# Gated mix of one decode step of cached attention and a feed-forward layer: from the tile framework to planned semaphores, with one TensorE loop over items, two key buffers and one value buffer

## The chip, the cores and the metric

The kernel runs on one core of a Trainium2 chip. The metric is the device time of one execution in microseconds (us). A core has five engines with instruction streams of their own: TensorE (PE in the profile; PEld are its weight loads), VectorE (DVE), ScalarE (ACT), GpSimd (POOL) and SyncE (SP). SP issues nearly all loads here, on one queue, which 16 DMA engines serve. An engine waits for another, or for a load, by a semaphore.

## The reference

All data is float32. B = 2 rows of x, D = 640, H = 32 heads of 128, 4096 cached positions, F = 1728.

```python
def _A_ref(x, k_cache, v_cache, wq, wo):            # x (2,1,640), caches (2,32,4096,128)
    q = (x @ wq).reshape(B, Sq, H, Dh)              # wq (640, 4096)
    scores = einsum("bhqd,bhkd->bhqk", q, k_cache) * Dh ** -0.5
    p = softmax(scores)
    o = einsum("bhqk,bhkd->bhqd", p, v_cache)
    return o.reshape(B, Sq, H * Dh) @ wo            # wo (4096, 640)

def _B_ref(x, w1, w2):                              # w1 (640, 1728), w2 (1728, 640)
    return silu(x @ w1) @ w2

g = sigmoid((x * gate_w).sum(-1))
out = g * _A_ref(...) + (1 - g) * _B_ref(...)
```

The caches are 268 MB of the 298 MB that are read.

## The kernel before

An *item* is four heads of one row of x: 16 items, `items[i] = (hq, b)`, with hq from 0 to 7 and b 0 or 1. For each item a key slab and a value slab of 128 partitions x 16384 floats (8.39 MB) are read. Everything large goes through three buffers of that size that rotate (`slabs`, SLOTS = 3): two loads with the query weights and w1, then keys and values, one load "mid" with w2 and the first two of eight groups of output weights, and at the very end "end" with the other six groups. The list `stream` sets the order, and all of them are issued on SP (`load` at L100, `load_wo` at L91). A load of the stream is issued once the one three places earlier has been used up (`spend`, `pump`): the framework makes it wait for the last reader of that buffer.

For an item, `products` multiplies the key slab by the query in place: VectorE the first 68 of 128 columns of 128 (L323), GpSimd the others (L320). `scores` sums them on VectorE (L331), `peak` finds each row's maximum (L336 to L340), and `weights` takes exponentials on ScalarE (L346) into `pz`, of which there are two. `total` and `values` run on TensorE: the sum of the exponentials (L357) and 32 products of 32 columns with the value slab (L372). `combine` scales the result on VectorE (L384) and picks each head's own part in one product (L394); `turn` adds and transposes once per pair of items (L405, L406). `project` multiplies by the output weights (L213): the groups up to the sixth into `early`, two strips of output partitions of 320 columns, and the last two into `acc`, four strips of 160; `merge` adds the first to the second. In program order an iteration holds item i's products and item i-1's values. The last value slab comes in two halves. At the end VectorE copies `acc` (L455), and SP and ACT store one row each (L457).

The queries of an item pair are spread over the partitions just before they are needed (`query`, L308), `ffn_in` and `query_rows` run at the start (L244, L291), and `ffn_out` after item 5 (`middle`).

Of the kernel before, what the change touches and what calls it, by code (L numbers as in the profile page):

```python
# [1 line left out]

# [12 lines left out]
@with_exitstack  # L15
def tile_gated_decode(
    ctx: ExitStack,
    tc: tile.TileContext,
    x: bass.AP,
    kc: bass.AP,  # L20
    vc: bass.AP,
    wq: bass.AP,
    wo: bass.AP,
    w1: bass.AP,
    w2: bass.AP,
    gate: bass.AP,
    out: bass.AP,
):
    nc = tc.nc
# [5 lines left out]
    Q = 4  # L35
# [5 lines left out]
    FR = F // P  # L41
    FM = FR * P
    FT = F - FM
    QF = FM // Q
    SLOTS = 3
    SLAB = C * DH
    QD = Q * DH

    const = ctx.enter_context(tc.tile_pool(name="const", bufs=1))
    slabs = ctx.enter_context(tc.tile_pool(name="slabs", bufs=SLOTS))  # L50
    work = ctx.enter_context(tc.tile_pool(name="work", bufs=2))
    ps_q = ctx.enter_context(tc.tile_pool(name="ps_q", bufs=1, space=bass.MemoryType.PSUM))
    ps_r = ctx.enter_context(tc.tile_pool(name="ps_r", bufs=1, space=bass.MemoryType.PSUM))
    ps_pv = ctx.enter_context(tc.tile_pool(name="ps_pv", bufs=2, space=bass.MemoryType.PSUM))
    ps_o = ctx.enter_context(tc.tile_pool(name="ps_o", bufs=1, space=bass.MemoryType.PSUM))
    ps_s = ctx.enter_context(tc.tile_pool(name="ps_s", bufs=3, space=bass.MemoryType.PSUM))
    order = ctx.enter_context(tc.manual_schedule())
# [4 lines left out]
    N = len(items)  # L62
    MID = 5
    J0 = SLAB // (H * DH)
    W1_AT = (J - J0) * H * DH
    XG_AT = W1_AT + J * F
    W2T_AT = FR * D
    WO_MID = 2
    WO_AT = {}
    for grp in range(HQ):  # L70
        WO_AT[grp] = ("mid", W2T_AT + D + grp * Q * D) if grp < WO_MID else ("end", (grp - WO_MID) * Q * D)
# [10 lines left out]
    T = {}  # L82
    spent = set()
    nxt = [0]

    def load_wo(grp, t):
        at = WO_AT[grp][1]
        src = wo[grp * QD : (grp + 1) * QD, :].rearrange("(p n) d -> p (n d)", n=Q)
        cuts = (0, Q * D - D, Q * D) if grp == HQ - 1 else (0, Q * D)
        for c0, c1 in zip(cuts, cuts[1:]):  # L90
            nc.sync.dma_start(t[:, at + c0 : at + c1], src[:, c0:c1])  # L91

    def load(what, n, t):
        if what in ("k", "v"):
            hq, b = items[n]
            src = (kc if what == "k" else vc)[b, Q * hq : Q * hq + Q]
            src = src.rearrange("h s d -> (h s d)").rearrange("(p c) -> p c", p=P)
            step = SLAB // 2 if (what, n) == ("v", N - 1) else SLAB
            for c in range(0, SLAB, step):
                nc.sync.dma_start(t[:, c : c + step], src[:, c : c + step])  # L100
        elif what == "wq":
            src = wq.rearrange("(p j) n -> p (j n)", j=J)
            if n == 0:
                nc.sync.dma_start(t, src[:, :SLAB])
            else:
                nc.sync.dma_start(t[:, :W1_AT], src[:, SLAB:])
                nc.sync.dma_start(t[:, W1_AT : W1_AT + J * F], w1.rearrange("(p j) f -> p (j f)", j=J))
        elif what == "mid":
            for grp in range(WO_MID):
                load_wo(grp, t)  # L110
            nc.sync.dma_start(t[:, : FR * D], w2[:FM, :].rearrange("(p n) d -> p (n d)", n=FR))
            nc.sync.dma_start(t[:FT, W2T_AT : W2T_AT + D], w2[FM:, :])
        else:
            for grp in range(WO_MID, HQ):
                load_wo(grp, t)

    def pump():
        while nxt[0] < len(stream):
            m = nxt[0]
            if m >= SLOTS and stream[m - SLOTS] not in spent:  # L120
                return
            t = slabs.tile([P, SLAB], F32, tag="slab", name=stream[m][0])
            load(*stream[m], t)
            T[stream[m]] = t
            nxt[0] += 1

    def spend(what, n):
        spent.add((what, n))
        pump()

    pump()
    xg = T["wq", 1][: B + 1, XG_AT : XG_AT + D]
    nc.scalar.dma_start(xg[:B], x.rearrange("b s d -> (b s) d"))
    nc.scalar.dma_start(xg[B : B + 1], gate[None, :])

    ident = const.tile([P, P], F32, name="ident")
    make_identity(nc, ident)
    ones = const.tile([P, P], F32, name="ones")  # L140
    nc.vector.memset(ones, 1.0)
    fold = const.tile([P, 2 * Q, Q, 4], F32, name="fold")
    nc.vector.memset(fold, 0.0)
    for q in range(Q):
        nc.vector.memset(fold[q * QP : (q + 1) * QP, :, q, :], 1.0)
    sel = const.tile([P, 4 * Q], F32, name="sel")
    nc.vector.reduce_sum(sel, ident.rearrange("p (a b) -> p b a", b=32)[:, : 4 * Q, :], axis=AX.X)
    pick = const.tile([P, P + 1], F32, name="pick")
    nc.vector.memset(pick, 0.0)
    nc.vector.reduce_sum(pick[:, 1 : P + 1 : 32], sel.rearrange("p (q c) -> p q c", c=4), axis=AX.X)  # L150
    own = const.tile([P, 4], F32, name="own")
    nc.vector.reduce_sum(own, sel.rearrange("p (q c) -> p c q", c=4), axis=AX.X)
    spread = const.tile([P, B, P], F32, name="spread")
    for b in range(B):
        for q in range(Q):
            nc.vector.tensor_copy(
                spread[:, b, q * QP : (q + 1) * QP],
                ident[:, 32 * q + b : 32 * q + b + 1].to_broadcast([P, QP]),
            )
    xz = const.tile([P, J, 32], F32, name="xz")  # L160
    nc.gpsimd.memset(xz, 0.0)
    pz = []
    for i in range(2):
        t = const.tile([P, NG, 32], F32, name=f"pz{i}")
        nc.gpsimd.memset(t, 0.0)
        pz.append(t)

    g = const.tile([P, B], F32, name="g")
    gc = const.tile([P, B], F32, name="gc")
    hT = const.tile([P, FR, B], F32, name="hT")  # L170
    hTt = const.tile([FT, 1, B], F32, name="hTt")

    def gates():
        xT = ps_s.tile([P, 512], F32, tag="sm", name="xT")
        for j in range(J):
            nc.tensor.matmul(  # L176
                xT[:, j * (B + 1) : (j + 1) * (B + 1)],
                xg[:, j:D:J],
                ident[: B + 1, : B + 1],
                start=True,  # L180
                stop=True,
            )
        xT = xT[:, : J * (B + 1)].rearrange("p (j r) -> p j r", j=J)
        nc.vector.tensor_copy(xz[:, :, :B], xT[:, :, :B])  # L184
        gx = const.tile([P, B, J], F32, name="gx")
        for b in range(B):
            nc.vector.tensor_mul(gx[:, b, :], xT[:, :, B], xz[:, :, b])
        gp = const.tile([P, B], F32, name="gp")
        nc.vector.reduce_sum(gp, gx, axis=AX.X)
        gl = ps_s.tile([P, 512], F32, tag="sm", name="gl")  # L190
        nc.tensor.matmul(gl[:, :B], ones, gp, start=True, stop=True)
        ge = const.tile([P, B], F32, name="ge")
        nc.scalar.activation(ge, gl[:, :B], AF.Exp, scale=-1.0)
        nc.vector.tensor_scalar_add(ge, ge, 1.0)
        nc.vector.reciprocal(g, ge)
        nc.vector.tensor_scalar(gc, g, -1.0, 1.0, op0=ALU.mult, op1=ALU.add)

    G = 4  # L200
    W = D // G
    W2 = D // 2
    LAST = HQ - 2
    both = ps_o.tile([P, W2 + W], F32, name="acc")
    early, acc = both[:, :W2], both[:, W2:]
    count = {"early": 0, "late": 0}
    total_of = {"early": Q * LAST + FR + 1, "late": Q * (HQ - LAST) + 1}

    def accumulate(lhsT, w, to="early"):
        m = lhsT.shape[1]  # L210
        dst, width = (early, W2) if to == "early" else (acc, W)
        for n in range(D // width):
            nc.tensor.matmul(  # L213
                dst[32 * n : 32 * n + m, :],
                lhsT,
                w[:, n * width : (n + 1) * width],
# [5 lines left out]
    def merge():  # L222
        part = const.tile([64, W2], F32, name="part")
        nc.scalar.copy(part, early[:64, :])
        for n in range(G):
# [6 lines left out]
                stop=False,  # L232
            )
        count["late"] += 1

    def ffn_in():
# [242 lines left out]
```

## Time and profile before

| | |
|---|---|
| three runs | 701.09, 701.51, 707.64 us (median 701.51) |
| span of the profiled execution | 700.5 us |
| its own time beside the span | not given apart; the runs' median lies 1.0 us above the span |
| read from memory | 298.26 MB |
| busy | DMA queue of SP 98.7%; DVE 67%, POOL 38%, PE 32%, ACT 5% |

The span runs from the first to the last instruction. In the timeline a row has the start, the length, the engine, the line, the operation, output and inputs, and in brackets the idle time before it with what ended it. In the chain of work that ended last a row has start, length and what. In the list of waits stand the waiter, what it waited for, the total, the number and the longest. "SPq" is SP issuing a load, "to landing" the time from issue until the data is there.

### The profile page before, as it was taken

How to read it: one execution, taken by the hardware profiler on the slowest of the kernel's cores; microseconds unless marked ns; L12 is line 12 of the kernel's file. 1: busy time of each engine (PE TensorE's matmuls, PEld its weight loads, DVE VectorE, ACT ScalarE, POOL GpSimd, SP SyncE). 2: the span in 40 equal slices, each digit the busy share in tenths (PEclk: the TensorE clock that was granted, in tenths of full speed). 3: DMA queues.
4: the chain of work that ended last, by engine and by line, in shares of the span. 5: the costliest groups of instructions: out<-in, count | busy, mean ns of one | idle time of the engine just before them, and what ended most of it. 6: DMA issues, size and time to landing. Idle time of an engine off the chain costs nothing.

```text
span 700.5 us, 3603 instructions
## 1 busy us (share of the span) xinstructions
PE 224.3 (32%) x1496; PEld 71.7 (10%) x1496; DVE 468.6 (67%) x212; ACT 37.8 (5%) x143; POOL 265.8 (38%) x25
## 2 busy tenths in 40 slices
PE   1630060506041240852240506050321406060467
PEld 1110010101010010210010102010100102010112
DVE  2016949494958869495949597795949495786901
ACT  0000000101010100101010101010010101010010
POOL 1006244270908163453618090724426080715300
PEclk9975565756657575877575757566565757566689
DMA  9999999999999999999999999999999999999995
GB/s 416 401 451 419 427 465 423 423 427 457 427 427 434 449 424 430 417 421 438 430 439 434 434 427 443 438 427 427 446 434 427 423 453 431 427 427 449 411 422 222
DMA packets 6742, 298.50 MB, mean 426 GB/s; under 512 B 763, under 2 KB 771, under 8 KB 1094
## 3 DMA queue, kind: packets, MB, share of 16 engines
q1 hardware_dynamic: 6712, 298.26, 98.7%
q8 instruction: 12, 0.20, 0.1%
q14 instruction: 4, 0.03, 0.0%
q10 hardware_dynamic: 14, 0.01, 0.0%
HBM read 298.26 MB, written 0.01 MB: 426 GB/s over the span
## 4 chain that ended last, share of the span: by engine, by line
DMA 59%; DVE 24%; PE 14%; another core or an unknown queue 1%; ACT 0%; issue 0%; SPq 0%; DVEq 0%; ACTq 0%
DMA k<-in_A_k_cache_dram 34%; DMA v<-in_A_v_cache_dram 20%; DVE s L331 15%; PE pv L372 10%; DVE k L323 8%; DMA wq<-in_B_w_dram 5%; PE acc L213 2%; PE orow L394 1%; PE hr L244 1%; DVE osb L384 0%; ACT pz L346 0%; PE tot L357 0%; DVE rg L365 0%; DVE m L336 0%
## 5 line engine op out<-in xcount | busy, mean ns | idle before, releaser
L320 POOL TENSOR_TENSOR k<-k,qsb 128x7680 f32<-128x7680 f32 x16 | 263.1, 16447 | 387.7 <-DMA k<-in_A_k_cache_dram 387.7
L331 DVE TENSOR_REDUCE s<-k 128x68 f32<-128x8704 f32 (+1 forms) x32 | 276.3, 8676 | 0.0
L323 DVE TENSOR_TENSOR k<-k,q 128x8704 f32<-128x8704 f32 x16 | 147.5, 9221 | 136.3 <-DMA k<-in_A_k_cache_dram 126.1
L372 PE MATMUL pv<-v,pz 128*32 128x512 f32 x1024 | 145.4, 731 | 248.1 <-DMA v<-in_A_v_cache_dram 248.1
L372 PEld LDWEIGHTS pv<-v,pz 128*32 128x32 f32 x1024 | 36.8, 131 | 342.8 <-issue 227.2
L394 PE MATMUL orow<-osb,pick 128*128 128x512 f32 x32 | 22.8, 800 | 118.2 <-DVE osb L384 118.2
L346 ACT ACTIVATE pz<-s,nb 32x128 f32<-32x128 f32 x64 | 25.5, 398 | 585.7 <-DVE nb L340 585.1
L384 DVE SCALAR_TENSOR_TENSOR osb<-pv,rg,own 128x512 f32<-128x512 f32 x16 | 12.0, 747 | 22.6 <-PE pv L372 22.6
L263 DVE STREAM_TRANSPOSE turned<-hr 128x416 f32<-128x416 f32 (+1 forms) x2 | 0.8, 408 | 30.6 <-PE hr L252 30.6
L357 PE MATMUL tot<-rs,fold 128*128 128x1 f32 x32 | 5.8, 250 | 43.2 <-ACT pz L346 43.2
L394 PEld LDWEIGHTS orow<-osb,pick 128*128 128x128 f32 x32 | 5.8, 226 | 127.9 <-DVE osb L384 127.9
L308 PE MATMUL q<-qrow,spread 128*128 128x128 f32 x32 | 7.2, 359 | 25.7 <-DVE tot L362 18.0
L291 PE MATMUL qr<-wq,xz 128*32 128x512 f32 x80 | 10.5, 683 | 9.2 <-DMA wq<-in_A_wq_dram 9.2
L405 DVE TENSOR_REDUCE row<-orow 128x128 f32<-128x512 f32 x8 | 5.5, 691 | 11.6 <-PE orow L394 11.6
L213 PE MATMUL acc<-mid,hT 128*2 128x320 f32 x52 | 10.1, 563 | 8.6 <-DMA mid<-in_B_w_dram 8.6
L357 PEld LDWEIGHTS tot<-rs,fold 128*128 128x128 f32 x32 | 7.2, 235 | 54.3 <-ACT pz L346 51.2
L346 ACT ACTIVATION_READ_ACCUMULATOR pz<-s,nb 32x1 f32 x64 | 11.8, 184 | 0.0
L213 PE MATMUL acc<-end,oP 128*2 128x320 f32 (+2 forms) x128 | 11.1, 366 | 0.0
L308 PEld LDWEIGHTS q<-qrow,spread 128*128 128x128 f32 x32 | 5.4, 239 | 32.6 <-issue 23.1
L244 PE MATMUL hr<-wq,xz 128*32 128x416 f32 x40 | 6.1, 744 | 5.0 <-DMA wq<-in_B_w_dram 5.0
L455 DVE COPY ot<-acc 128x160 f32<-128x160 f32 x1 | 0.3, 323 | 11.0 <-PE acc L213 11.0
L184 DVE COPY xz<-xT 128x10 f32<-128x10 f32 x1 | 0.2, 169 | 9.1 <-PE xT L176 9.1
(55 smaller groups left out, 65.8 us busy)
## 6 DMA issues: line engine op xcount, KB each, us to landing
v<-in_A_v_cache_dram SPq DMA_DIRECT2D x2, 4096.0 KB, 38.3
end<-in_A_wo_dram SPq DMA_DIRECT2D x5, 1280.0 KB, 21.0
wq<-in_B_w_dram SPq DMA_DIRECT2D x1, 4320.0 KB, 37.6
mid<-in_B_w_dram SPq DMA_DIRECT2D x1, 4160.0 KB, 27.9
mid<-in_A_wo_dram SPq DMA_DIRECT2D x2, 1280.0 KB, 17.5
wq<-in_A_wq_dram SPq DMA_DIRECT2D x1, 2048.0 KB, 26.7
end<-in_A_wo_dram SPq DMA_DIRECT2D x1, 960.0 KB, 26.8
end<-in_A_wo_dram SPq DMA_DIRECT2D x1, 320.0 KB, 27.1
```

What stands on the lines that cost most here:

```text
L213: nc.tensor.matmul(dst[32 * n : 32 * n + m, :], lhsT, w[:, n * width : (n + 1) * width], start=(count[to] == 0), stop=(count[to] == total_ ...
L244: nc.tensor.matmul(rows[32 * c : 32 * c + 32, :QF], xz[:, j, :], w[:, j, c * QF : (c + 1) * QF], start=(j == 0), stop=(j == J - 1),)
L291: nc.tensor.matmul(ps[u][32 * q : 32 * q + 32, :], xz[:, j, :], w[:, u * half : (u + 1) * half, q, :], start=(j == 0), stop=(j == J - 1),)
L308: nc.tensor.matmul(qps[hq][:, b, :], spread[:, b, :], qrow[:, hq, :], start=True, stop=True)
L320: nc.gpsimd.tensor_mul(k[:, CV:, :], k[:, CV:, :], qsb[hq][:, b, None, :].to_broadcast([P, C - CV, DH]))
L323: nc.vector.tensor_mul(k[:, :CV, :], k[:, :CV, :], qps[hq][:, b, None, :].to_broadcast([P, CV, DH]))
L331: nc.vector.reduce_sum(S[i][:, c0:c1], k[:, c0:c1, :], axis=AX.X)
L346: nc.scalar.activation(pz[i % 2][lo:hi, :, 4 * q : 4 * q + 4], S[i][lo:hi].rearrange("p (g c) -> p g c", c=4), AF.Exp, bias=M[i][lo:hi], s ...
L357: nc.tensor.matmul(t[:, :1], fold.rearrange("p a q c -> p (a q c)"), R[i], start=True, stop=True)
L372: nc.tensor.matmul(PV[i][32 * q : 32 * q + 32, :], pz[i % 2][:, gr, :], v[:, gr, :], start=(gr < 4), stop=(gr >= NG - 4),)
L384: nc.vector.scalar_tensor_tensor(osb, PV[i].rearrange("p (c d) -> p c d", d=DH), R[i], own[:, :, None].to_broadcast([P, 4, DH]), op0=ALU.mult,
L394: nc.tensor.matmul(PO[hq].rearrange("p c d -> p (c d)"), pick[:, 1 - b : P + 1 - b], osb.rearrange("p c d -> p (c d)"), start=(b == 0), st ...
```

## The change

The kernel is written anew without the tile framework. The computation is split over the engines as before (68 of 128 columns on VectorE, 32 value products per item on TensorE), but:

- A class `Planner` keeps for each engine a semaphore that counts its operations and puts a wait ahead of an operation where a name that it reads or writes was last written or read elsewhere. All loads go through `dma` (L113 after).
- Three fixed buffers: `ka` and `kb` hold keys of even and odd items, `va` holds values. Key slab i+2 waits for item i's sums, value slab i for item i-1's value products.
- w2 is loaded at the start into `va` and used there (`add_early`, four strips of 320 columns), its rows as 128 x 8640 in one load. The queries of all heads are spread once and stay in four PSUM banks and in `qsb`.
- TensorE's work per item is one hardware loop of 16 turns (L474 after): the sum of the exponentials, the 32 value products, then eight products of 128 columns that pick each head's part. ScalarE and VectorE hand over through `s_w` and `s_o`. There is one `pz`, one `pv`, one `osb`. `turn` transposes after each item.
- All output weights are loaded after the last value slab, 10.49 MB: three groups of eight heads into `ka`, the fourth, in three pieces, into `kb`. The first three groups go into `early` on four strips, the fourth into four strips of 160. The last value slab is not split.

```diff
-    stream = [("wq", 0), ("wq", 1)]
-    for i in range(N):
-        if i <= MID:
-            stream += [("k", i), ("v", i)]
-        elif i == MID + 1:
-            stream += [("k", i), ("mid", 0)]
-        else:
-            stream += [("k", i), ("v", i - 1)]
-    stream += [("v", N - 1), ("end", 0)]
...
+    p.dma("sp", va[:, : FH * HALF], w2s, "l_w2", writes=["va"])
...
+        if what == "k":
+            name = "ka" if i % 2 == 0 else "kb"
+            p.dma("sp", keys[i % 2], src, f"l_k{i}", writes=[name] + (["wq1", "w1"] if i == 1 else []))
+        else:
+            p.dma("sp", va, src, "l_v", writes=["va"])
...
+    with t.Fori(0, N):
+        t.wait_ge(s_w, 1).then_inc(s_w, -1)
+        t.matmul(misc[:, 100:101], fold, rs, start=True, stop=True).then_inc(p.sem["pe"], 1)
+        t.wait_ge(p.sem["l_v"], 16).then_inc(p.sem["l_v"], -16)
+        for gr in range(NG):
+            q = gr % 4
+            m = t.matmul(
+                pv[32 * q : 32 * q + 32, :],
+                pz[:, gr, :],
+                pv_v[:, gr, :],
+                start=(gr < 4),
+                stop=(gr >= NG - 4),
+            )
+        m.then_inc(p.sem["pe"], 1)
+        t.wait_ge(s_o, 1).then_inc(s_o, -1)
+        for e in range(2):
+            for c in range(4):
+                m = t.matmul(
+                    po[:, e * DH : (e + 1) * DH],
+                    pk[:, 4 * e + c, :],
+                    osb[:, c * DH : (c + 1) * DH],
...
+                )
+        m.then_inc(p.sem["pe"], 1)
...
+    def looped(i):
+        p.looped(pe_count(i, 1), reads=["rs", "nb", f"s{i % 2}"], writes=["misc"])
+        p.looped(pe_count(i, 2), reads=["pz"], writes=["pv", "va"])
...
+    load("k", 0)
+    load("k", 1)
     for i in range(N + 1):
         if i < N:
             products(i)
         if i >= 1:
...
             invert(i - 1)
...
         if i < N:
             scores(i)
+            load("v", i)
+            if i + 2 < N:
+                load("k", i + 2)
             peak(i)
             weights(i)
...
         if i >= 1:
             combine(i - 1)
...
+            turn(i - 1)
+        if i < N:
+            looped(i)
...
+        for n0, n1 in zip(cuts, cuts[1:]):
+            name = f"wo{grp}_{n0}"
+            wo_names[grp, n0] = name
+            if (grp, n0) in ((0, 0), (NGR - 1, 0)):
+                p.wait("sp", p.needs("sp", [], [slab_name]))
+            p.dma("sp", slab[:, off + n0 * D : off + n1 * D], src[:, n0 * D : n1 * D], "l_" + name, writes=[name])
...
+                lambda n=n, h=h: add_early(
+                    2 * (n % 2) + h,
+                    op[:, grp, n, :],
+                    slab[:, off + n * D + h * HALF : off + n * D + (h + 1) * HALF],
+                )
```

What SP issues at the end, before: the rows from key slab 14 on. In brackets stand the semaphores that a row waits for (DMAHW: an earlier load; PE, DVE: an engine).

```order
L100 DMA k<-in_A_k_cache_dram 128x16384 [waits DMAHW1_49,PE_49]
L100 DMA v<-in_A_v_cache_dram 128x16384 [waits DMAHW2_49,DVE_49]
L100 DMA k<-in_A_k_cache_dram 128x16384 [waits DMAHW3_49,PE_49]
L100 DMA v<-in_A_v_cache_dram 128x16384 [waits DMAHW4_49,DVE_49]
L100 DMA v<-in_A_v_cache_dram 128x8192 [waits DMAHW5_49,PE_49]
L100 DMA v<-in_A_v_cache_dram 128x8192
L91 DMA end<-in_A_wo_dram 128x2560 [waits DMAHW6_49,DVE_49]
L91 DMA end<-in_A_wo_dram 128x2560 x4
L91 DMA end<-in_A_wo_dram 128x1920 [waits DMAHW7_49]
L91 DMA end<-in_A_wo_dram 128x640 [waits DMAHW0_49]
```

And SP's end after the change, from key slab 14 on; done_pe and done_dve count the operations of TensorE and VectorE.

```order
L113 DMA key_a<-in_A_k_cache_dram 128x16384 [waits done_dve]
L113 DMA val<-in_A_v_cache_dram 128x16384 [waits done_pe]
L113 DMA key_b<-in_A_k_cache_dram 128x16384 [waits done_dve]
L113 DMA val<-in_A_v_cache_dram 128x16384 [waits done_pe] x2
L113 DMA key_a<-in_A_wo_dram 128x5120 [waits done_dve]
L113 DMA key_a<-in_A_wo_dram 128x5120 x2
L113 DMA key_b<-in_A_wo_dram 128x3200 [waits done_dve]
L113 DMA key_b<-in_A_wo_dram 128x1280
L113 DMA key_b<-in_A_wo_dram 128x640
```

Before, the last value slab stands behind value slab 14 in another buffer and waits for item 13's products; now value slabs 14 and 15 stand one behind the other in `val`, each waiting for TensorE's products of the item ahead of it, and all output weights behind them.

What TensorE does with the output weights at its end, before: four groups of 320 columns, then the last two of 160 (`oP` holds the attention's result of a group).

```order
L213 MATMUL acc<-end,oP_710 2x320 [waits DMAHW2_49]
L213 MATMUL acc<-end,oP_710 2x320 x7
L213 MATMUL acc<-end,oP_842 2x320 [waits DMAHW3_49]
L213 MATMUL acc<-end,oP_842 2x320 x7
L213 MATMUL acc<-end,oP_974 2x320 [waits DMAHW4_49]
L213 MATMUL acc<-end,oP_974 2x320 x7
L213 MATMUL acc<-end,oP_1106 2x320 [waits DMAHW5_49]
L213 MATMUL acc<-end,oP_1106 2x320 x7
```

And after, from the end of its loop on (`op` holds the attention's result, `bank` is early's PSUM bank, then pv's):

```order
L439 MATMUL bank<-key_a,op 2x320 [waits l_wo0_0]
L439 MATMUL bank<-key_a,op 2x320 x15
L439 MATMUL bank<-key_a,op 2x320 [waits l_wo1_0]
L439 MATMUL bank<-key_a,op 2x320 x15
L439 MATMUL bank<-key_a,op 2x320 [waits l_wo2_0]
L439 MATMUL bank<-key_a,op 2x320 x15
L666 MATMUL bank<-key_b,op 2x160 [waits l_wo3_0,done_dve]
L666 MATMUL bank<-key_b,op 2x160 x19
L666 MATMUL bank<-te,small 2x160 [waits done_act]
L666 MATMUL bank<-te,small 2x160 x3
L666 MATMUL bank<-key_b,op 2x160 [waits l_wo3_5]
L666 MATMUL bank<-key_b,op 2x160 x7
```

The 32 wide products before are 48 now (and turn over four strips where they used two), because none of the output weights has been used earlier; 32 narrow ones follow, the last four of them behind the last piece of weights.

More of the change, by code (lines that the diff above doesn't have):

```diff
@@ L30, in tile_gated_decode, with gated_decode @@
+def gated_decode(nc, x, kc, vc, wq, wo, w1, w2, gate, out):
     P = 128
@@ L83, in tile_gated_decode @@
[L83 to L104, printed above, removed]
-            else:
[L106 to L135, printed above, removed]
@@ L148, in tile_gated_decode @@
[L148 to L196, printed above, removed]
@@ L200, in tile_gated_decode @@
[L200 to L216, printed above, removed]
-                start=(count[to] == 0),
-                stop=(count[to] == total_of[to] - 1),
-            )
-        count[to] += 1
@@ L305, in query @@
-    def query(hq):
-        qps[hq] = ps_q.tile([P, B, DH], F32, name="q")
-        for b in range(B):
-            nc.tensor.matmul(qps[hq][:, b, :], spread[:, b, :], qrow[:, hq, :], start=True, stop=True)
-        qsb[hq] = work.tile([P, B, DH], F32, name="qsb", bufs=1)
-        nc.scalar.copy(qsb[hq], qps[hq])
-    CV = 68
-    S, M, R, PV, PO, OP = {}, {}, {}, {}, {}, {}
-    def products(i):
-        hq, b = items[i]
-        k = T["k", i].rearrange("p (c d) -> p c d", d=DH)
-        nc.gpsimd.tensor_mul(
-            k[:, CV:, :], k[:, CV:, :], qsb[hq][:, b, None, :].to_broadcast([P, C - CV, DH])
-        )
-        nc.vector.tensor_mul(
-            k[:, :CV, :], k[:, :CV, :], qps[hq][:, b, None, :].to_broadcast([P, CV, DH])
-        )
@@ new lines, in gated_decode @@
+    osb = sb("osb", [P, QD])
+    pk = sb("pk", [P, 8, P])
+    op = sb("op", [P, NGR, GH, B])
+    hl = sb("hl", [P, FH, 2 * B])
+    te = sb("te", [P, FE, 32])
+    to = sb("to", [P, FO, 32])
+    ident = sb("ident", [P, P])
+    ones = sb("ones", [P, P])
+    spread = sb("spread", [P, B, P])
+    fold = sb("fold", [P, P])
+    xq = sb("xq", [P, J, B, 32])
+    xg = sb("xg", [B + 1, D])
+    he = sb("he", [P, FH, B])
+    sel = sb("sel", [P, 16])
+    small = sb("small", [P, 64])
+    sums = sb("sums", [P, 2, C])
@@ new lines, in gated_decode @@
+    for j in range(J):
+        p.group("pe", query(j), reads=["xq", "ka" if j < J - 1 else "wq1"], writes=["pv", "po"])
+    p.op("act", lambda: a.copy(qrow[:, 0], pv), reads=["pv"], writes=["qrow0"])
+    p.op("dve", lambda: v.tensor_copy(qrow[:, 1], po), reads=["po"], writes=["qrow1"])
+    for u in range(2):
+        p.group(
+            "pe",
+            [
+                lambda b=b: t.matmul(qps[u * B + b], spread[:, b, :], qrow[:, u, :], start=True, stop=True)
+                for b in range(B)
+            ],
+            reads=["spread", f"qrow{u}"],
+            writes=["qps"],
+        )
@@ new lines, in gated_decode, with ffn_in @@
+    for i in range(4):
+        p.op(
+            "act",
+            lambda i=i: a.copy(qsb[:, i // B, i % B], qps[i]),
+            reads=["qps"],
+            writes=["qsb", "qrow0", "qrow1"],
+        )
+    rows = po[:, :FQ]
+    def ffn_in(j):
+        w = kb[:, W1_AT : W1_AT + J * F].rearrange("p (j f) -> p j f", j=J)
+        lhsT = xq[:, j].rearrange("p b r -> p (b r)")[:, 16:48]
+        return [
+            lambda c=c: t.matmul(
+                rows[32 * c : 32 * c + 32, :],
+                lhsT,
+                w[:, j, c * FQ : (c + 1) * FQ],
+                start=(j == 0),
+                stop=(j == J - 1),
+            )
+            for c in range(Q)
+        ]
@@ new lines, in gated_decode @@
+    for j in range(J):
+        p.group("pe", ffn_in(j), reads=["xq", "w1"], writes=["po"])
+    for dst, name, off, step in ((te, "te", 0, FO), (to, "to", 0, FE)):
+        n = dst.shape[1]
+        src = bass.AP(
+            tensor=rows.tensor,
+            offset=rows.offset,
+            ap=[list(rows.ap[0]), [1, n], [FH, FQ // FH], [step, 2]],
+        )
+        p.op(
+            "dve",
+            lambda dst=dst, src=src: v.transpose(dst, src),
+            reads=["po"],
+            writes=[name],
+        )
@@ new lines, in gated_decode, with add_early @@
+    for k, (m, name) in enumerate(((gce, "gce"), (gco, "gco"))):
+        p.op(
+            "dve",
+            lambda k=k, m=m: v.tensor_mul(
+                hl[:, :, k * B : (k + 1) * B], he, m[:, None, :].to_broadcast([P, FH, B])
+            ),
+            reads=["he", name],
+            writes=["hl"],
+        )
+    started = set()
+    def add_early(strip, lhsT, rhs):
+        m = lhsT.shape[1]
+        first = strip not in started
+        started.add(strip)
+        return t.matmul(
+            early[32 * strip : 32 * strip + m, :HALF], lhsT, rhs, start=first, stop=False, skip_group_check=True
+        )
@@ L420, in middle @@
-    def middle():
-        for grp in range(WO_MID):
-            project(grp)
-        ffn_out()
-        spend("mid", 0)
-    gates()
-    query_rows()
-    query(0)
-    ffn_in()
+        m.then_inc(p.sem["pe"], 1)
[6 more added lines that the diff above has]
+                    osb[:, c * DH : (c + 1) * DH],
+                    start=(e == 0 and c == 0),
+                    stop=(c == 3),
+                    skip_group_check=True,
+                )
@@ new lines, in weights, with one @@
+    def weights(i):
+        s, tag = sums[:, i % 2], f"s{i % 2}"
+        def one(q):
+            lo, hi = q * QP, (q + 1) * QP
+            return a.activation(
+                pz[lo:hi, :, 4 * q : 4 * q + 4],
+                s[lo:hi].rearrange("p (g c) -> p g c", c=4),
+                AF.Exp,
+                bias=nb[lo:hi],
+                scale=SCALE,
+                accum_out=rs[lo:hi],
+            )
+        p.group("act", [lambda q=q: one(q) for q in range(Q - 1)], reads=[tag, "nb"], writes=["pz", "rs"])
+        p.handed("act", lambda: one(Q - 1), s_w, reads=[tag, "nb"])
```

660 lines of the change are left out of this document (440 added, 220 removed).

## The prediction

> **What bounds the kernel now.** I read the page's busy shares and slices first.
>
> ```profile
> span 700.5 us, 3603 instructions
> PE 224.3 (32%) x1496; PEld 71.7 (10%) x1496; DVE 468.6 (67%) x212; ACT 37.8 (5%) x143; POOL 265.8 (38%) x25
> DMA  9999999999999999999999999999999999999995
> q1 hardware_dynamic: 6712, 298.26, 98.7%
> ```
>
> No engine computes for more than 67% of the span, while the one load queue moves its 298.26 MB in 98.7% of it. The waits agree: TensorE, VectorE and GpSimd stand idle for slabs.
>
> ```profile
> POOL k L320 <- DMA k<-in_A_k_cache_dram: 387.7, 16, 55.4
> PE pv L372 <- DMA v<-in_A_v_cache_dram: 248.1, 10, 28.5
> DVE k L323 <- DMA k<-in_A_k_cache_dram: 126.1, 15, 11.1
> ```
>
> So the time is bytes over rate, plus what lies outside the stream, plus every stretch in which the queue has nothing to move. The rate is in the chain that ended last: VectorE starts on a key slab when it lands.
>
> ```profile
> 213.14 9.22 DVE k L323
> ...
> 327.13 9.22 DVE k L323
> ...
> 443.00 9.22 DVE k L323
> ...
> 558.83 9.22 DVE k L323
> ```
>
> From 443.00 to 558.83 lie six slabs of 8.39 MB: 115.83 us, **19.3 us a slab**, 434.6 GB/s. From 213.14 to 327.13 lie five slabs and the "mid" load (7.05 MB): 114.0 less 96.5 leaves 17.5 for what should take 16.2, so that load's small pieces cost 1.3 us.
>
> The end is in the timeline.
>
> ```profile
> 656.97 9.28 PE L372 MATMUL pv<-v,pz 128*32 128x512 f32 x64 [26.72 <-DMA v<-in_A_v_cache_dram]
> 676.20 6.47 PE L372 MATMUL pv<-v,pz 128*32 128x512 f32 x32 [4.27 <-DMA v<-in_A_v_cache_dram]
> 684.60 9.05 PE L213 MATMUL acc<-end,oP 128*2 128x320 f32 x72
> 694.59 2.08 PE L213 MATMUL acc<-end,oP 128*2 128x160 f32 x56
> 625.83 3.17 SPq L100 DMA_DIRECT2D v<-in_A_v_cache_dram  x3
> 664.39 3.45 SPq L91 DMA_DIRECT2D end<-in_A_wo_dram  x7
> end<-in_A_wo_dram SPq DMA_DIRECT2D x1, 320.0 KB, 27.1
> ```
>
> Value slab 14 lands at 656.97, the last half of slab 15 at 676.20. Both were issued between 625.83 and 629.0, so the queue never ran out. The last output weights were issued at about 667.4 and landed 27.1 us later, at 694.5; TensorE, busy since 676.20 with hardly a break, ends at 696.67, 2.2 us behind the last byte. The remaining 3.8 us are the final copy and the store.
>
> **The change, part by part.**
>
> *The last value slab.* The order of issues shows two value loads back to back at the end, each into the one buffer "val", each waiting for TensorE. Slab 15 can't be issued until item 14's products have read slab 14, and no key slab lies between them. The output weights stand behind slab 15 on SP, though their key buffers are long free. So the queue runs dry when slab 14 lands. The dry stretch is item 14's products, the 9.28 us above. Elsewhere the same 64 instructions (two for each product in the code) took between these two:
>
> ```profile
> 243.94 7.61 PE pv L372 x64
> ...
> 88.89 10.02 PE pv L372 x64
> ```
>
> TensorE will have waited some 26 us for the slab, as it had before the 9.28 (26.72 idle), so I take that. Then the empty queue starts again. The nearest row is the kernel's first slab.
>
> ```profile
> 0.73 0.39 SPq L104 DMA_DIRECT2D wq<-in_A_wq_dram  x1
> wq<-in_A_wq_dram SPq DMA_DIRECT2D x1, 22.3
> ```
>
> It took 22.3 us from issue to landing against 19.3 in the full stream, so a restart costs 3.0. The restart could cost nothing (19.3) if that excess belongs to the program's start; I take 22.3, the only slab here that met an empty queue. From landing 14 to landing 15: 9.3 + 22.3 = 31.6 instead of 19.2, **+12.4 us**; between 7.6 + 19.3 (+7.7) and 10.0 + 22.3 (+13.1).
>
> The Trainium skill, "DMA: Bandwidth & Descriptors", section "Anatomy of one DMA", fits one transfer as about 2.0 us fixed plus its bytes at 436 GB/s, on another issue path. By that slab 15 would take an estimated 21.2 us and the term would be 1.1 us smaller; the row of 22.3 decides here.
>
> *The moved weights.* Two pieces of 1280 KB leave the middle and join the end: slab 14 lands 2.62 MB / 434.6 GB/s = 6.0 us earlier and the tail is 6.0 longer, together nothing. The feed-forward rows (4.42 MB) go to the start, bytes unchanged. The 1.3 us that "mid" lost may go or may move with them: I take −0.65, keep −1.3 and 0.
>
> *The steady state.* Does the single value buffer also stall each of the other items? Order: k(i), v(i−1), k(i+1), v(i). With k(i) landing at T, v(i−1) lands at T+19.3, its products end at T+28.7, v(i) is issued then and is wanted at T+38.6: a lead of 9.9 us, with key slab i+1 as cover. Slab i+2's issue waits for item i's sums.
>
> ```profile
> 558.83 9.22 DVE L323 TENSOR_TENSOR k<-k,q 128x8704 f32<-128x8704 f32 x1 [6.16 <-DMA k<-in_A_k_cache_dram]
> 568.31 17.27 DVE L331 TENSOR_REDUCE s<-k 128x68 f32<-128x8704 f32 x2
> 587.69 0.75 DVE L384 SCALAR_TENSOR_TENSOR osb<-pv,rg,own 128x512 f32<-128x512 f32 x1 [1.06 <-PE pv L372]
> DMA to landing us min/median/max: 29.2/31.1/45.9
> ```
>
> The sums end 26.8 us after landing, so k(i+2) goes out right behind v(i), 29 us before it is wanted. The last row is the value slabs' time from issue to landing now: 29.2 at the least, also a lead of 9.9, and the stream held 19.3 a slab with it. Cost: 0. The trace of before has no hardware loop, so what an iteration of TensorE's loop adds is unknown; up to 9.9 us of it are covered, and each us beyond costs 14, once for each of the other value loads but the first.
>
> VectorE gains per item a wait for eight 128-row products (16 instructions) and a small transpose. Four such instructions took 0.71:
>
> ```profile
> 33.56 0.71 PE L308 MATMUL q<-qrow,spread 128*128 128x128 f32 x4
> ```
>
> So 2.8 us, or 5.7 at half the granted clock, which most slices come near:
>
> ```profile
> PEclk9975565756657575877575757566565757566689
> ```
>
> Behind VectorE's wait stands the next item's multiply, which waits for its slab until T+38.6; VectorE is through at T+28.7, plus 0.8 for the scaling, 5.7, and 1.3 allowed for transpose and copy (an estimate from the scaling's 0.75 for twice the columns): T+36.5. Cost: 0.
>
> *The start.* Key slab 0 now needs the query weights' buffer, and slab 1 the buffer of the feed-forward input. The same consumers release today's second and third cache loads:
>
> ```profile
> 31.97 0.33 SPq L100 DMA_DIRECT2D v<-in_A_v_cache_dram  x1
> 45.48 0.33 SPq L100 DMA_DIRECT2D k<-in_A_k_cache_dram  x1
> 58.57 9.22 DVE L323 TENSOR_TENSOR k<-k,q 128x8704 f32<-128x8704 f32 x1 [10.15 <-DMA k<-in_A_k_cache_dram]
> ```
>
> The first three loads plus w2 keep the queue busy until 58.57 − 19.3 + 10.2 = 49.5, later than both. Value slab 0 waits for w2's products (54 instructions, under 8 us by the 9.05 for 72), and two key slabs cover those. Cost: 0.
>
> *The end.* After slab 15 come 10.49 MB, 24.1 us. TensorE needs 9.3 for the products, 0.8 for VectorE's scaling, 2.8 for the rows, then 96 instructions of width 320 for the first 24 heads. Before, these used two strips of output partitions, 0.141 us each (9.05 for 64, rest of the row 160 wide); the last part used four, 2.08 / 56 = 0.037 at half the width. The new code turns over four strips: 2 × 0.037 × 96 = 7.1. That ends 20.0 after slab 15; the next piece lands at 24.1 − 2.3 = 21.8. So the weights end last and only eight instructions follow the last byte: 0.5 instead of 2.2, **−1.7**. If four strips were no faster, 13.5 in place of 7.1, then the last part's 72 instructions (2.7): 29.1 after slab 15 instead of 24.8, +4.3.
>
> ```profile
> SPq L477 <- DMA out_dram<-ot: 1.2, 2, 0.9
> SPq L477 <- PEq L477: 1.1, 2, 0.9
> ```
>
> The first row is the wait for the store, which stays as an explicit wait. The second is the framework's closing exchange between engines, which goes: worth nothing to 1 us, and I take nothing, since the runtime's own end is not in the trace.
>
> *Sum.* Slab 14 lands at 656.97 − 6.0 − 0.65 = 650.3; products to 659.6; slab 15 at 681.9; last weights at 706.0, with 0.2 for the 694.5 measured against 676.2 + 18.1: 706.2; last product 706.7; end 706.7 + 3.8 = **710.5 us of span**, 10.0 above the 700.5. The runs' median of 701.51 stands 1.0 above the span, so the time is **711.5**.
>
> **The rivals.**
>
> *The single buffer stalls every item.* The Trainium skill, "Trainium Kernel Development and Optimization", section "Best Practices", asks for double buffers so that transfer and work overlap. As a mechanism here: if products plus loop overhead outlast the lead of 9.9 us by 5 us, 14 items pay it: 70 us, about 781. For it: val is one buffer. Against: k(i+1) is the second transfer that covers it, and 29.2 shows that lead to be enough.
>
> *TensorE ends last,* from the two-strip rate above: 711.5 + 4.3 = 716. For it: TensorE ended last before. Against: 0.037 for half the width at four strips.
>
> *Not slower, because the stream gets faster.* If something that leaves (scattered small loads, the framework's extra waits) now slows each slab, all 35.6 slab-lengths gain. It decides from 0.28 us a slab on, 10.0 / 35.6 or 1.5%: at 19.0 the time is 701.5. Against: the rate is the same whatever runs beside it. The Trainium skill, "DMA: Bandwidth & Descriptors", section "Specifications", puts the ceiling of the path into SBUF at 435 GB/s, an estimated 19.28 a slab; by that rule this rival can't happen, and the trace, at 19.3, agrees.
> *It isn't what its words say:* the order could be rearranged so that the dry stretch vanishes; the order of issues excludes that.
>
> **How the numbers follow.** Forecast 0.80 (706 to 713), every item 0.05, TensorE last 0.08, faster stream 0.04, a dry stretch at its low bound with all gains (700.5 + 7.7 − 1.7 − 1.3 − 1 + 1 = 705.2) 0.03. The range 705.5 to 716.5 holds the forecast's unknowns and the TensorE case; outside lie the every-item case and the faster stream. One per cent, 7 us, is about what a measurement here can tell from none. Slower by over 1% means above 708.5: most of the forecast, less its low corner, and two rivals: 0.83. Within 1%: 0.13. Faster: 0.04.
>
> **What would show it.** After: a wait of SP for TensorE's products before the last value load, one or two slices with DMA well under 9 near the end, 31 to 32 us between the landings of the last two value slabs, and 24 from there to the last weights. Wrong would be: SP's other value loads issued less than 2 us before the stream needs them, DMA digits under 9 in the middle, or TensorE busy without a break up to the end.

## The result, and the profile after

The changed kernel takes **712.0 us** (median of four runs; 711.28 to 712.64) against 701.3 for the kernel before. The ratio on record is 1.0136, 95% interval 1.0096 to 1.0176: slower by 1.4%, where 711.5 us was forecast. The two medians alone give 1.0153; one of the four runs of the kernel before took 707.64 us, the others 701.06 to 701.51. The profiled execution took 711.28 us, its span 710.0.

The page of the changed kernel: span, busy shares, the slices with the share of the DMA engines, and the load queue.

```profile
span 710.0 us, 3940 instructions
PE 242.7 (34%) x1674; PEld 113.9 (16%) x1674; DVE 558.5 (79%) x234; ACT 36.7 (5%) x138; POOL 264.3 (37%) x23
DMA  9999999999999999999999999999999999993996
q1 hardware_dynamic: 6056, 298.26, 97.2%
```

The same 298.26 MB, and every slice at 9 but two: the 37th, from 639 to 657 us, and the last. Before, only the last one fell. The other number that moved is VectorE's, 558.5 us of work where it had 468.6.

The timeline of SP and of TensorE around that slice (start, length, engine, line):

```profile
618.33 40.11 SPq L113 DMA_DIRECT2D val<-in_A_v_cache_dram  x2
658.48 1.48 SPq L113 DMA_DIRECT2D key_a<-in_A_wo_dram  x3
672.34 1.29 SPq L113 DMA_DIRECT2D key_b<-in_A_wo_dram  x3
...
648.37 9.69 PE L480 MATMUL bank<-val,pz 128*32 128x512 f32 x64 [8.85 <-PEq L477]
679.99 8.77 PE L480 MATMUL bank<-val,pz 128*32 128x512 f32 x64 [2.06 <-PEq L477]
689.72 2.02 PE L491 MATMUL bank<-osb,pk 128*128 128x128 f32 x16 [0.96 <-PEq L488]
691.67 4.49 PE L439 MATMUL bank<-key_a,op 128*2 128x320 f32 x64
698.12 2.33 PE L439 MATMUL bank<-key_a,op 128*2 128x320 f32 x32 [1.96 <-DMA key_a<-in_A_wo_dram]
703.44 1.54 PE L666 MATMUL bank<-key_b,op 128*2 128x160 f32 x40 [2.98 <-DMA key_b<-in_A_wo_dram]
705.06 1.08 PE L666 MATMUL bank<-key_b,op 128*2 128x160 f32 x24
```

SP's first row holds two loads: value slab 14 at 618.33, and slab 15, whose row ends at 658.44, so its 0.33 us issue began at 658.11. In between SP waits. TensorE starts on slab 14 at 648.37, reads it until 658.06, and 0.05 us later slab 15 goes out. TensorE starts on that one at 679.99, 31.6 us after slab 14. From 648 to 658 us nothing moves (last columns: TensorE's clock, DMA share, GB/s):

```profile
648.00:658.00 10.00, 9.63 (x64) 2.70 (x64) 9.96 (x4) 0.00 (x0) 0.00 (x0) 0.72 0.00 0
```

The end is the weights' now: the last piece, issued at 673.2, took 32.5 us and landed at 705.7, and TensorE was done with it 0.5 us later, at 706.14.

```profile
key_b<-in_A_wo_dram SPq DMA_DIRECT2D x1, 320.0 KB, 32.5
```

The stream itself runs as before, 38.60 us for a pair of slabs (GpSimd starts on a key slab when it lands):

```profile
590.39 16.42 POOL L514 TENSOR_TENSOR key_a<-key_a,qsb 128x7680 f32<-128x7680 f32 x1 [22.21 <-DMA key_a<-in_A_k_cache_dram]
628.99 16.45 POOL L514 TENSOR_TENSOR key_b<-key_b,qsb 128x7680 f32<-128x7680 f32 x1 [22.18 <-DMA key_b<-in_A_k_cache_dram]
```

VectorE's extra work is one instruction that the prediction had at under 1.3 us together with a transpose. From the groups, the copy's tile (least, median and longest in ns, first and last start), then the timeline of VectorE:

```profile
L602 DVE COPY op<-to 64x8 f32<-64x8 f32 x16 | 88.2, 5515 | 0.5
...
L602 DVE COPY op<-to x16: 169/5619/14361, 128.9 to 692.3; 64x8 f32<-64x8 f32 x16
...
639.82 5.65 DVE L602 COPY op<-to 64x8 f32<-64x8 f32 x1
645.39 9.20 DVE L520 TENSOR_TENSOR key_b<-key_b,bank 128x8704 f32<-128x8704 f32 x1
...
678.35 0.17 DVE L602 COPY op<-to 64x8 f32<-64x8 f32 x1
```

A copy of 8 columns takes 5.65 us while GpSimd multiplies and ends when GpSimd does (628.99 + 16.45 = 645.44); with GpSimd idle it takes 0.17. VectorE's lag begins with item 0's copy: the first two key slabs land 19.3 us apart, VectorE is late after them, and the copy at 128.9, the longest of all, stands 14.36 us, up to the end of GpSimd's multiply of the third slab (126.82 to 143.26). The copies of items 1 to 13 then fall into the next multiply each. From the third key slab on, VectorE therefore starts on each one 16.4 us after it lands and no longer waits for any; what idle time it has left per item is some 3.9 us ahead of the transpose, for TensorE's rows (the eight products that pick each head's part).

### The profile page after: what moved, and what is told of

Its sections match the earlier page's. It is cut to its first block, busy times and chain, and to the rows that moved or that the text cites. A ratio compares the mean times of both kernels' runs of the same rounds, so it can differ in the third digit from the quotient of the medians.

```text
span 710.0 us, 3940 instructions
## 1 busy us (share of the span) xinstructions
PE 242.7 (34%) x1674; PEld 113.9 (16%) x1674; DVE 558.5 (79%) x234; ACT 36.7 (5%) x138; POOL 264.3 (37%) x23
## 3 DMA queue, kind: packets, MB, share of 16 engines
q1 hardware_dynamic: 6056, 298.26, 97.2%
HBM read 298.26 MB, written 0.01 MB: 420 GB/s over the span
## 5 line engine op out<-in xcount | busy, mean ns | idle before, releaser
L514 POOL TENSOR_TENSOR key_a<-key_a,qsb 128x7680 f32<-128x7680 f32 x8 | 131.3, 16418 | 222.2 <-DMA key_a<-in_A_k_cache_dram 222.2
L480 PE MATMUL bank<-val,pz 128*32 128x512 f32 x1024 | 146.4, 736 | 144.0 <-PEq L477 144.0
L514 POOL TENSOR_TENSOR key_b<-key_b,qsb 128x7680 f32<-128x7680 f32 x8 | 131.4, 16425 | 158.1 <-DMA key_b<-in_A_k_cache_dram 158.1
L491 PE MATMUL bank<-osb,pk 128*128 128x128 f32 x256 | 57.1, 414 | 242.6 <-PEq L488 242.6
L532 DVE TENSOR_REDUCE sums<-key_a 128x68 f32<-128x8704 f32 (+1 forms) x16 | 138.9, 8682 | 0.9
L532 DVE TENSOR_REDUCE sums<-key_b 128x68 f32<-128x8704 f32 (+1 forms) x16 | 138.9, 8681 | 0.8
L491 PEld LDWEIGHTS bank<-osb,pk 128*128 128x128 f32 x256 | 53.5, 319 | 256.6 <-issue 256.6
L520 DVE TENSOR_TENSOR key_a<-key_a,bank 128x8704 f32<-128x8704 f32 x8 | 73.7, 9212 | 22.5 <-DMA key_a<-in_A_k_cache_dram 22.4
L602 DVE COPY op<-to 64x8 f32<-64x8 f32 x16 | 88.2, 5515 | 0.5
L520 DVE TENSOR_TENSOR key_b<-key_b,bank 128x8704 f32<-128x8704 f32 x8 | 73.7, 9211 | 0.1
## 6 DMA issues: line engine op xcount, KB each, us to landing
key_b<-in_A_wq_dram SPq DMA_DIRECT2D x1, 2048.0 KB, 26.3
key_b<-in_A_wo_dram SPq DMA_DIRECT2D x1, 320.0 KB, 32.5
```

The source lines that it names most:

```text
L480: m = t.matmul(pv[32 * q : 32 * q + 32, :], pz[:, gr, :], pv_v[:, gr, :], start=(gr < 4), stop=(gr >= NG - 4),)
L491: m = t.matmul(po[:, e * DH : (e + 1) * DH], pk[:, 4 * e + c, :], osb[:, c * DH : (c + 1) * DH], start=(e == 0 and c == 0), stop=(c == 3), ...
L514: lambda: gp_eng.tensor_mul(k[:, CV:, :], k[:, CV:, :], qs[:, None, :].to_broadcast([P, C - CV, DH])),
L520: lambda: v.tensor_mul(k[:, :CV, :], k[:, :CV, :], qp[:, None, :].to_broadcast([P, CV, DH])),
L532: lambda c0=c0, c1=c1: v.reduce_sum(s[:, c0:c1], k[:, c0:c1, :], axis=AX.X),
L602: lambda: v.tensor_copy(op[lo : lo + 64, hq // 2, :, b], turned[lo : lo + 64, :, 0]),
```

## The experiments

The theory: the dry queue at the last value slab costs the time. Rivals: the longer stretch of weights behind that slab, VectorE as the new bound, and a single value buffer that stalls in the stream.

**VectorE's lag alone (e1_copy_act).** In `turn`:

```diff
-            "dve",
-            lambda: v.tensor_copy(op[lo : lo + 64, hq // 2, :, b], turned[lo : lo + 64, :, 0]),
+            "act",
+            lambda: a.copy(op[lo : lo + 64, hq // 2, :, b], turned[lo : lo + 64, :, 0]),
```

> The small copy of each item's result goes from VectorE to ScalarE, nothing else. In the changed kernel's profile that copy took 5.5 us in the mean on VectorE (88 us in all) and ended each time when GpSimd's multiply ended, which left VectorE without idle time. Theory: the copy waits for GpSimd, and VectorE's lag is covered by the key slabs' lead. Then VectorE's busy time falls from 558 to about 473 us, the copy takes under 0.6 us, the key slabs' time from issue to landing grows from 33.8 to about 48 us, and the time stays at 711 to 713. Rival: VectorE without idle time is the new bound; then the time falls by 5 to 10 us. Rival: the copy is slow by its shape; then it takes some 5 us on ScalarE too.

Measured: 712.3 us (712.04 to 712.53), 1.0153 of the kernel before (1.0138 to 1.0169). The page, the copy's tile, the loads of keys (last column: issue to landing), and the issue and the last piece of the fourth group of weights:

```profile
PE 220.1 (31%) x1674; PEld 90.4 (13%) x1674; DVE 472.0 (66%) x218; ACT 39.9 (6%) x154; POOL 264.8 (37%) x23
L602 ACT COPY op<-to x16: 199/202/206, 129.0 to 692.3; 64x8 f32<-64x8 f32 x16
key_a<-in_A_k_cache_dram SPq DMA_DIRECT2D x8, 47.9
659.80 1.49 SPq L113 DMA_DIRECT2D key_b<-in_A_wo_dram  x3
key_b<-in_A_wo_dram SPq DMA_DIRECT2D x1, 320.0 KB, 44.5
```

The copy takes 0.20 us on ScalarE, the first one (129.0) while GpSimd multiplies (127.18 to 143.63), so its shape is not slow. VectorE loses 86.5 us of work, and key slabs go out 14 us earlier. The time doesn't move. The changed kernel's chain of work that ended last does run through VectorE: its sums for item 15 release the fourth group of weights at 672.34. Here that group goes out at 659.80, 12.5 us earlier, and its last piece still lands only at 705.3 (705.7 in the changed kernel). VectorE's lag lies wholly within the lead of the loads and is not what made the kernel slower.

**The dry stretch alone (e2_last_buffer).** The last value slab goes into a buffer that is free; the weights stay last:

```diff
-            p.dma("sp", va, src, "l_v", writes=["va"])
+            if i == N - 1:
+                p.dma("sp", ka, src, "l_vl", writes=["ka"])
+            else:
+                p.dma("sp", va, src, "l_v", writes=["va"])
...
-    with t.Fori(0, N):
+    with t.Fori(0, N - 1):
+        turn_of_pe(pv_v, "l_v")
+    turn_of_pe(ka.rearrange("p (g c) -> p g c", g=NG), "l_vl")
...
-        return (kb, 0, "kb") if grp == NGR - 1 else (ka, grp * GH * D, "ka")
+        return (kb, 0, "kb") if grp == NGR - 1 else (va, grp * GH * D, "va")
```

> The last value slab goes into key buffer a, free by then, so that it need not wait for item 14's products; the first three groups of output weights go into the value buffer; TensorE's last turn stands behind the loop. The weights are still all last. Theory (dry queue): value slab 15 lands 19 to 20 us after slab 14 instead of 31.6, no slice near the end falls under 9, the last weights land at about 692 instead of 705.7. But VectorE's lag now shows: item 15's sums end at 672, so its value products start at about 678 and TensorE ends last, at about 700: span about 704, time about 705. Rival (the longer stretch of weights behind the last value slab costs the time): nothing changes, 711 to 713.

Measured: 703.3 us (701.85 to 703.71), 1.0019 of before (1.0010 to 1.0028). Of the 10.7 us that the changed kernel lost, 8.7 are gone with the weights still last, which ends the rival that blames their length. The time is 1.7 us below the expected 705. The page's slices, then rows of SP's timeline, of the loads (issue to landing), of the same ten microseconds, and of VectorE's and TensorE's timelines:

```profile
DMA  9999999999999999999999999999999999999993
633.87 0.33 SPq L113 DMA_DIRECT2D key_a<-in_A_v_cache_dram  x1
key_a<-in_A_v_cache_dram SPq DMA_DIRECT2D x1, 33.8
648.00:658.00 10.00, 9.18 (x64) 2.54 (x64) 9.96 (x4) 0.00 (x0) 0.00 (x0) 0.76 0.98 426
654.99 17.47 DVE L541 TENSOR_REDUCE sums<-key_b 128x68 f32<-128x8704 f32 x2
678.22 7.99 PE L483 MATMUL bank<-key_a,pz 128*32 128x512 f32 x64
697.23 1.00 PE L675 MATMUL bank<-key_b,op 128*2 128x160 f32 x24
```

Slab 15 lands at 633.87 + 33.8 = 667.7, but its products start at 678.22: item 15's sums end only at 672.5, VectorE being late by its copies. TensorE then ends last, at 698.2.

**Both (e3_both).** The two edits above together.

> Last value slab in key buffer a, as in the run with that alone, and the small copy on ScalarE. Theory: item 15's sums end at about 658, its value products start when its slab lands at 668, TensorE has done the first three groups before the last weights land at 692, and the span is about 692 + 4.3 = 696, time about 697 to 698: below the kernel before (701.3). Rival (VectorE's lag plays no part): as with the buffer alone, 705, or 711 to 713 if the dry queue is not the cause.

Measured: **697.7 us** (697.51 to 697.91), 0.9945 of before (0.9931 to 0.9958): faster than both kernels. TensorE's timeline:

```profile
648.83 9.75 PE L483 MATMUL bank<-val,pz 128*32 128x512 f32 x64 [26.96 <-PEq L480]
668.13 8.64 PE L483 MATMUL bank<-key_a,pz 128*32 128x512 f32 x64 [6.44 <-PEq L480]
686.24 2.34 PE L439 MATMUL bank<-val,op 128*2 128x320 f32 x32 [2.07 <-DMA val<-in_A_wo_dram]
690.14 1.54 PE L675 MATMUL bank<-key_b,op 128*2 128x160 f32 x40 [1.56 <-DMA key_b<-in_A_wo_dram]
691.77 1.01 PE L675 MATMUL bank<-key_b,op 128*2 128x160 f32 x24
```

Slab 15 comes 19.3 us after slab 14, one slab's length. The copy, worth nothing in e1, is worth 5.6 us here: with the dry stretch gone, VectorE's lag was what came next.

**Cover without a buffer (e4_cover).** The first two groups of weights are issued ahead of the last value slab:

```diff
+    AHEAD = 2
...
+            if i == N - 1:
+                for grp in range(AHEAD):
+                    load_wo(grp)
             load("v", i)
```

> One value buffer as in the changed kernel, but the first two groups of output weights (5.24 MB, 12.1 us) are issued ahead of the last value slab, as cover for item 14's products. Theory (dry queue): the queue stays full, slab 15 lands at about the same time as in the changed kernel (680), since its wait is now filled with weights, and only 5.24 MB follow it: the last weights land at 692 instead of 705.7. TensorE then ends last: products 688.6, rows 691.7, first three groups 698.4, last group 701.3, span about 705, time about 706. Rival (the restart and the wait cost nothing, bytes behind the slab do): the gain is the whole 12.1 us, time 700.

Measured: 706.6 us (705.50 to 706.75), 1.0067 of before (1.0052 to 1.0083). The page's slices, then rows of SP's and TensorE's timelines:

```profile
DMA  9999999999999999999999999999999999999992
634.39 0.80 SPq L113 DMA_DIRECT2D key_a<-in_A_wo_dram  x2
658.84 0.33 SPq L113 DMA_DIRECT2D val<-in_A_v_cache_dram  x1
680.80 8.77 PE L480 MATMUL bank<-val,pz 128*32 128x512 f32 x64 [2.18 <-PEq L477]
692.49 6.64 PE L439 MATMUL bank<-key_a,op 128*2 128x320 f32 x96
700.57 1.00 PE L673 MATMUL bank<-key_b,op 128*2 128x160 f32 x24
```

Slab 15 is issued and lands within a microsecond of where it did in the changed kernel, but the wait before it is filled: no slice but the last falls under 9. TensorE, whose weight products all stand behind its loop, ends last at 701.6. That the gain is 5.4 us and not the 12.1 of the moved bytes was expected from this chain.

**Less lead (e5_lead).** On top of e1, a value load waits for the rows of the item before too (the eight products behind the value products):

```diff
-        p.looped(pe_count(i, 2), reads=["pz"], writes=["pv", "va"])
+        p.looped(pe_count(i, 2), reads=["pz"], writes=["pv"])
+        p.looped(pe_count(i, 3), writes=["va"])
```

> On top of the run with the copy on ScalarE (712.3): each value load waits until the rows of the item before (eight products behind VectorE's scaling) are done, not only its value products. That takes 0.8 + 0.1 + 2.0 to 3.7 us from the lead of some 10 us with which value slabs are issued. Theory: a lead of 6 to 7 us still keeps the queue full, so key slabs land 38.6 us apart as before, the value slabs' time from issue to landing falls from 29.4 to about 25.5 to 26.5, and only the dry stretch at the end grows, by about 3 us: time 715 to 716. Rival (the lead is already at its limit, the single value buffer stalls in the stream): 14 loads lose 3 us or more each, time 750 or more.

Measured: 719.5 us (718.81 to 720.36), 1.0256 of before (1.0239 to 1.0273), 4 us more than expected. Value slabs, issue to landing (least, median, most), then SP's timeline and the DMA share near the start:

```profile
DMA to landing us min/median/max: 21.9/26.3/51.5
128.65 0.33 SPq L113 DMA_DIRECT2D val<-in_A_v_cache_dram  x1
125.00:130.00 5.00, 3.84 (x18) 3.75 (x18) 1.34 (x2) 1.27 (x7) 3.03 (x1) 0.60 0.47 157
```

In the stream the theory holds: a lead of 26.3 − 19.3 = 7.0 us is enough, and key slabs land 38.6 to 38.7 us apart from the fourth on, but for one at 39.2. The expectation missed one place. The first two key slabs come right behind one another, so VectorE is late, item 0's rows are done only at 128.6, when key slab 2 has landed already, and value slab 1 meets an empty queue: key slab 3 comes 4.4 us later than in e1. The last slab's gap grows by 3.1 us, as expected.

**More dry stretches (e6_pairs).** The changed kernel with two key slabs and then two value slabs:

```diff
-            load("v", i)
-            if i + 2 < N:
-                load("k", i + 2)
+            if i % 2:
+                load("v", i)
+                for n in (i + 1, i + 2):
+                    if n < N:
+                        load("k", n)
+            else:
+                load("v", i)
```

> The changed kernel with the loads in another order: two key slabs, then two value slabs, so that each second value slab stands directly behind the first one, as the last one does in the changed kernel. Eight dry stretches instead of one. Theory: each costs the products (about 9.3 us) and the restart (2.4 in the last slab's own landing, up to 4.2 with what the weights behind it lost): seven more give 82 to 95 us, time 794 to 807; the value slabs fall in two kinds, 22 us from issue to landing and about 60. Rival (the end of the changed kernel is late for another reason): 712.

Measured in one execution: 795.7 us. The page's slices, two of TensorE's rows and one of GpSimd's:

```profile
DMA  9999949997699939997799959996699939997795
...
642.01 9.45 PE L480 MATMUL bank<-val,pz 128*32 128x512 f32 x64 [5.94 <-PEq L477]
673.51 8.77 PE L480 MATMUL bank<-val,pz 128*32 128x512 f32 x64 [2.12 <-PEq L477]
692.78 16.43 POOL L514 TENSOR_TENSOR key_a<-key_a,qsb 128x7680 f32<-128x7680 f32 x1 [53.75 <-DMA key_a<-in_A_k_cache_dram]
```

The slices show the holes along the whole span. The second value slab of the pair shown comes 31.5 us after the first (30.4 to 31.8 over the eight pairs), much the same gap as at the changed kernel's end, and seven more gaps cost 795.7 − 712.0 = 83.7 us, 12.0 each. The key slab behind it lands 19.3 us later (673.51 to 692.78), one slab's length, so nothing more is lost there. The first value slabs of the pairs took 48 to 52 us from issue to landing, not about 60.

**The kernel before once more (e7_before_again).** No edit. It took 701.5 us, with a span of 699.7.

> The kernel before, unchanged, for a second trace. In the first one key slab 14 landed 40.1 us after key slab 13, against 38.6 for the other pairs, and the pair with the small loads of mid took 1.3 us more than its bytes ask for. If the 1.5 us is a chance of that execution, it is gone or elsewhere now; the 1.3 us of mid should stand again.

```profile
559.21 16.43 POOL L320 TENSOR_TENSOR k<-k,qsb 128x7680 f32<-128x7680 f32 x1 [22.20 <-DMA k<-in_A_k_cache_dram]
598.92 16.45 POOL L320 TENSOR_TENSOR k<-k,qsb 128x7680 f32<-128x7680 f32 x1 [23.27 <-DMA k<-in_A_k_cache_dram]
```

Key slab 14 again comes 39.7 us after slab 13, 1.1 more than a pair's 38.6 (1.5 in the first trace): not a chance of one execution. The pair with "mid" loses 1.4 again. The changed kernel has neither; what delays key slab 14 in the kernel before is open.

## Why the prediction was right

- **The dry stretch:** 31.6 us between the last two value slabs foretold, 31.62 measured (9.3 + 22.3 against 9.69 and 21.7 with 0.2 around them). That the terms' small misses cancel to nothing is chance. e2 and e3 show it as the cause, e6 its price elsewhere. A restart cost 2.4 us on the slab itself, 21.7 against 19.3. The Trainium skill, "DMA: Bandwidth & Descriptors", section "Anatomy of one DMA", in its fit for another issue path, puts such a slab at an estimated 21.2 us; the measurement lies between this and the row of 22.3 that was taken.
- **The stream before it** was mis-sized: −0.65 for "mid", measured −2.6 (slab 14 at 648.37, not 650.3). In the changed kernel neither the 1.3 us of "mid" nor the 1.5 of key slab 14 stands, 2.8 together; the prediction had left out the second.
- **The weights behind the last slab** were mis-sized the other way: 24.1 + 0.2 foretold, 25.7 measured (679.99 to 705.7). In e3, where no dry stretch lies ahead, the same bytes took 24.2 (668.1 to 692.3). The rows show where the 1.5 us went: TensorE starts on the fourth group 5.3 us after the third (698.12 and 703.44), in e3 3.9 (686.24 and 690.14). So the loss lies there and not behind the restart in general, and in e6 a key slab behind a restart lost nothing. e1, which issues that group 12.5 us earlier, doesn't bring it in sooner; what holds it up is open.
- **Luck:** the last two misses, of the stream and of the weights, cancel but for 0.5 us: the span is 710.0 where the sum gave 710.5. The 1.0 us beside the span was wrong too, since it set the runs' median against the span of a single execution. Where both are on record for the same execution, the kernel before stands at least 1.7 us above its span (701.5 and 699.7 in e7), the changed kernel 1.3 to 1.4. So the closeness of 711.5 to 712.0 is partly chance.
- **The end:** four strips at 4.49 / 64 = 0.070 us an instruction (0.074 foretold), 0.5 us of work behind the last byte, as foretold. The load of the weights ended last, and TensorE waited for it.
- **The steady state** cost nothing, as foretold, but one step to it was wrong, the one that has VectorE through at T+36.5. It was never through ahead of the next slab, since the copy was priced by its size and not by what runs beside it, and the lag that the first two key slabs leave on VectorE was not counted. For an item on schedule the step is not far off: in e1, where no copy stands, VectorE waits 5.6 to 7.4 us for each key slab from the fourth on (6.06 for the last), so it is through at about T+32.5. That the lag cost nothing was luck: the key slabs' lead of 29 us was long enough and shrank only to 33.8 − 19.3 = 14.5. At the end only 2.1 us were left (TensorE's 2.06 us wait before item 15's products).
- Of the rivals, none came: the single value buffer stalls only where no key slab stands between two value loads.

## What to carry to other kernels

Here a single value buffer was enough wherever another slab was queued behind the one that was being used up, even with the lead cut to 7.0 us (e5), but for one place at that run's start, where the other slab had already landed. Look for the places in the issue order where two loads of one buffer are neighbours, above all at the end of a loop, where the other stream runs out first. The price there was the consumer's time plus a restart, about 12 us, paid once per neighbour pair (e6), so it could be worked out from two rows. When such a stretch is mended, look at once for the engine that it had been hiding: here the mend was worth 9 us alone and 14 with a copy moved that by itself was worth nothing.

## What the runs showed of the hardware that was not expected

A VectorE copy of 64 x 8 floats within the on-chip memory stood 5.5 us in the mean, up to the end of GpSimd's multiply, and counts as busy in the profile; beside no GpSimd work it took 0.17 us, and on ScalarE 0.21 us beside GpSimd. In e6 the copies that found GpSimd idle took 0.16 to 0.17 us, the seven others 2.7 to 3.1, again up to the end of GpSimd's multiply. VectorE's long multiply, which reads one operand from PSUM, ran beside GpSimd's in 9.2 us in the kernel before and in e1. The Trainium skill, "SBUF — State Buffer", section "SBUF: two separate sides", says that a VectorE operation in a two-port mode and a GpSimd operation lock each other out of one shared pair of ports for a whole instruction, and that a float32 copy within SBUF enters such a mode. The times agree with it, though no trace shows the mode itself; the prediction should have used it.
